# Four PSUM slots of two banks for attention, each read out for two products at once

## The chip, the cores and the metric

The kernel runs on one core of one Trainium2 chip. The metric is the device time of the program in microseconds (us). TensorE (PE) multiplies into PSUM, which has eight banks of 512 fp32 columns for each of its 128 partitions; VectorE (DVE) and ScalarE (ACT) read PSUM, GpSimd (POOL) works on the on-chip memory alone, and SyncE (SP) issues DMAs.

## The reference

Causal attention with a decay bias, for 8 batches, 8 heads, 576 positions and 64 dimensions per head; then a real part of a two-dimensional Fourier transform, a normalisation and a feed-forward layer with 2048 hidden units.

```python
scores = scale * np.matmul(q, k.transpose(0, 1, 3, 2))
cum = np.cumsum(np.maximum(s, 0.0), axis=-1)
bias = -(cum[:, :, :, None] - cum[:, :, None, :])
scores = np.where(causal, -1e9, scores + np.minimum(bias, 0.0))
scores = scores - np.max(scores, axis=-1, keepdims=True)
attn = np.exp(scores)
x = (attn / (attn.sum(-1, keepdims=True) + 1e-9)) @ v     # then heads side by side: (8, 576, 512)
u = x + np.real(np.fft.fft(np.fft.fft(x, axis=1), axis=2))
un = (u - mean(u)) / np.sqrt(var(u) + 1e-6)
out = u + np.maximum(un @ w_ch1, 0.0) @ w_ch2
```

## The kernel before

**The attention loop.** Two heads are one pair; there are 32 pairs (i), four to a batch. Iteration i of the loop does several things at once, as generators that `weave` mixes by the shares of work done: `scores(i)`, `maxes(i + 1)`, `av(i - 1)`, the preparation of the next operands (`high`, `low`), the finishing of older pairs (`recip`, `finish`), the folds and the Fourier transform (`fourier`) of an earlier batch, and a part of the conversion of the weights. TensorE's instructions keep the order in which they are written (`manual_schedule`); those of the other engines are placed by a scheduler and then run in order on each. Queue by queue, an instruction that waits holds up all behind it.

**Maxima (`maxes`).** For each head, five blocks of 128 queries (the last 64) are multiplied with all earlier keys into PSUM (tile pm, L459). The widths are 256, 256, 384 and 512 columns, and the last block takes two products of 256 and 320 columns. DVE adds the causal mask and takes the maximum of each row in one operation (L466; a second short instruction reads its accumulator); for the last block's first product it is a plain reduction (L462). The ten maxima of a pair are transposed on TensorE (pmt, L471), copied by ACT (L473) and sent by DMA into a row of the operand, so that the scores come out with the maximum taken off.

**Scores (`scores`).** Products of keys by queries, in chunks of 128 keys (table `CH`: first key, first query, number of queries, first query that counts). Each has two matmuls, one for the rounded operands and one for what the rounding left (tile ps, L491 and L492). The widths are 256 and 320 (chunk 0 in two parts), 448, 320, 256 and 256 columns; of the last two only 192 and 64 columns count. ACT takes the exponential of each into P (L495), six per head. POOL sets to zero what lies above the diagonal (L498, L501).

**Product with V (`av`).** In two column ranges, 256 (pavA) and 320 (pavB), with two and five matmuls (L523), one pass of P per chunk of keys. ACT copies each range out after its last matmul: once for the first head (L529), twice for the second (L526 for the row of sums, L527).

**PSUM.** The pool `ps` has three buffers of one bank and serves the scores, the Fourier transform, the normalisation and the hidden layer (`bank`). The pool `psm` has five and serves pm, pmt, pavA and pavB; it is closed before the feed-forward part, where four banks become the accumulators `accp`. A buffer is handed out again when its last reader is done.

**Other names.** L435 (k) subtracts the rounded keys on DVE, L438 (q) the queries on POOL; L83 to L89 convert the weights; L251 to L270 fold a batch for the transform; L284 to L336 are the transform (pzs, pzc, pyc, pys, p256) and L69 and L70 split its results; L183 is the first feed-forward product.

Of the kernel before, what the change touches and what calls it, by code (L numbers as in the profile page):

```python
# [8 lines left out]
F32 = mybir.dt.float32  # L9
# [10 lines left out]
S = 576  # L20
# [15 lines left out]
CH = [(0, 0, 576, 0), (128, 128, 448, 128), (256, 256, 320, 256), (384, 320, 256, 384), (448, 320, 256, 512)]  # L36
# [5 lines left out]
def fused_kernel(ctx, tc, qkT, vA, sP, wP, tabD, tabS, corr, out):  # L42
# [304 lines left out]
    psm = attb_ctx.enter_context(tc.tile_pool(name="psm", bufs=5, space=PSUM))  # L347
# [46 lines left out]
    trash = att.tile([128, 512], BF16, name="trash")  # L394
# [51 lines left out]
    def maxes(i):  # L446
        st = sts[i]
        qy, ky = st["qy"], st["ky"]
        M = Ms[i % 2]
        M1 = att.tile([128, 4], F32, tag="M1", name="M1", bufs=2)  # L450
        for h in range(2):
            for c in range(5):
                nq = 128 if c < 4 else 64
                nk = 128 * c + nq
                parts = [(0, max(nk, 256))] if c < 4 else [(0, 256), (256, 320)]
                col = M[:nq, 5 * h + c:5 * h + c + 1]
                for x, (k0, n) in enumerate(parts):
                    p = psm.tile([128, 512], F32, tag="m", name="pm", bufs=5)
                    nc.tensor.matmul(p[:, :n], qy[:, h, 128 * c:128 * c + 128], ky[:, h, k0:k0 + n], start=True, stop=True)  # L459
                    if len(parts) > 1 and not x:  # L460
                        first = M1[:nq, h:h + 1]
                        nc.vector.tensor_reduce(out=first, in_=p[:nq, :n], axis=AX.X, op=ALU.max)  # L462
                    else:
                        n = nk - k0
                        m0 = 512 - 128 * c + k0
                        nc.vector.tensor_tensor_reduce(out=trash[:nq, :n], in0=p[:nq, :n], in1=amask[:nq, m0:m0 + n], scale=1.0,  # L466
                                                       scalar=first if x else NEG, op0=ALU.add, op1=ALU.max, accum_out=col)
                    yield 1.0
        yield 3
        p = psm.tile([128, 512], F32, tag="m", name="pmt", bufs=5)  # L470
        nc.tensor.transpose(out=p[0:10, 0:128], in_=M, identity=ident)  # L471
        mt = att.tile([10, 128], F32R, tag="mt", name="mt", bufs=2)
        nc.scalar.copy(mt, p[0:10, 0:128])  # L473
# [3 lines left out]
    SCORES = 2 * 1600  # L477

    def scores(i):
# [3 lines left out]
        for h in range(2):  # L483
            P = attb.tile([128, PW], F32, tag="P", name="P", bufs=4)
            st["P"].append(P)
            for c, (k0, q0, nq, qk) in enumerate(CH):
                ksl = slice(k0, k0 + 128)
                parts = [(0, 256), (256, 320)] if c == 0 else [(q0, nq)]
                for a, n in parts:
                    p = bank("ps")  # L490
                    nc.tensor.matmul(p[:, :n], ky[:, h, ksl], qy[:, h, a:a + n], start=True, stop=False)  # L491
                    nc.tensor.matmul(p[:, :n], k1[:, h, ksl], q1[:, h, a:a + n], start=False, stop=True)  # L492
                    lo = max(a, qk)
                    o = POFF[c] + lo - qk
                    nc.scalar.activation(P[:, o:o + a + n - lo], p[:, lo - a:n], AF.Exp, scale=0.125)  # L495
                    if c == 3:
                        d4 = bass.AP(tensor=P.tensor, offset=P.offset, ap=[list(P.ap[0]), [576, 4], [1, 128]])
                        nc.gpsimd.affine_select(out=d4, in_=d4, pattern=[[0, 4], [1, 128]], compare_op=ALU.is_ge, fill=0.0, base=0, channel_multiplier=-1)  # L498
                    if c == 4:
# [6 lines left out]
    def av(i):  # L506
# [5 lines left out]
        for h in range(2):  # L512
            P = st["P"][h]
            vs = slice(64 * h, 64 * h + 128)
            for lo, n, tg in ((0, 256, "A"), (256, 320, "B")):
                p = psm.tile([128, 512], F32, tag="m", name="pav" + tg, bufs=5)
                cs = [c for c in range(5) if CH[c][3] < lo + n]
                for c in cs:
# [4 lines left out]
                    nc.tensor.matmul(p[:, a - lo:n], va[:, c, vs], P[:, o:o + w], start=c == 0, stop=c == cs[-1])  # L523
                    if c == cs[-1]:
                        if h:
                            nc.scalar.copy(r1[:, lo:lo + n], p[0:1, :n])  # L526
                            nc.scalar.copy(x[64:128, lo:lo + n], p[64:128, :n])  # L527
                        else:
                            nc.scalar.copy(x[:, lo:lo + n], p[:, :n])  # L529
# [107 lines left out]
    w1 = ctx.enter_context(pool("w1"))  # L637
    accp = ctx.enter_context(pool("accp", space=PSUM))
# [174 lines left out]
```

## Time and profile before

| | |
|---|---|
| median of the runs, us | 1428.55 (1426.3 to 1429.79, 3 runs) |
| the profiled execution, us | 1426.1, of which its span is 1424.4 |
| granted TensorE clock, mean | 0.97 |
| attention loop, from the start to about | 540 us |
| end of attention, first loads of weights | 540 to 720 us |
| feed-forward part | 720 us to the end |

The page gives busy time by engine, by slice and by group of instructions; the waits name the engine and line that waited, and the engine and line that ended the wait. A matmul's duration runs from its start to the end of its write, and matmuls overlap, so the distance of two starts is what one of them costs TensorE. An fp32 product (L523) shows as two matmuls.

### The profile page before, as it was taken

What the parts mean: (1) busy time and instruction counts of PE and PEld (TensorE: products, weight loads), DVE (VectorE), ACT (ScalarE), POOL (GpSimd) and SP (SyncE); (2) the same over time, 40 slices, a digit from 0 to 9 for tenths busy, and PEclk for the clock granted to TensorE, in tenths of its full rate; (3) what the DMA queues carried; (4) which work ended last, traced back from release to release, by engine and by line L of the source; (5) the groups of instructions that cost most, each with busy time, mean ns of one, the idle gap of its engine ahead of it and who ended that gap; (6) DMA issues with size and microseconds to landing.
All of it is one profiled execution on the core that took longest, in us unless ns stands there. A gap on an engine that the chain in (4) does not pass through costs nothing.

```text
span 1424.4 us, 17997 instructions
## 1 busy us (share of the span) xinstructions
PE 1305.1 (92%) x6190; PEld 1068.7 (75%) x6190; DVE 745.7 (52%) x1684; ACT 539.3 (38%) x1211; POOL 561.6 (39%) x543
## 2 busy tenths in 40 slices
PE   4887979897988887997899999999999999999998
PEld 3766868686777676775688888888888888888886
DVE  6667677877777788799833233222332223322212
ACT  4775756676665656344321121211212112121110
POOL 6445465656546566565720402204022040123300
PEclk9998999999999997999899999999999999999999
DMA  8555556565655555433200000000000000000000
GB/s 214 156 159 144 163 149 180 158 168 159 159 161 144 166 149 163 162 123 121 79 8 30 31 30 15 15 30 31 30 15 15 30 30 30 15 16 0 30 0 30
DMA packets 78230, 125.05 MB, mean 88 GB/s; under 512 B 11256, under 2 KB 36249, under 8 KB 78139
## 3 DMA queue, kind: packets, MB, share of 16 engines
q1 hardware_dynamic: 75627, 119.83, 28.4%
q0 software_dynamic: 1696, 2.50, 0.9%
q10 hardware_dynamic: 816, 1.57, 0.3%
q8 instruction: 49, 0.80, 0.2%
q14 instruction: 42, 0.34, 0.1%
HBM read 76.85 MB, written 23.07 MB: 70 GB/s over the span
## 4 chain that ended last, share of the span: by engine, by line
PE 51%; DVE 7%; POOL 2%; DMA 1%; issue 1%; ACT 1%; SPq 0%; DVEq 0%; POOLq 0%; ACTq 0%
PE h L183 25%; PE acc L198 8%; PE acc L196 8%; PE acc L197 8%; POOL we L89 1%; DVE wm L88 1%; DVE we L83 1%; DVE wm L85 1%; DVE we L87 1%; DVE wl L114 1%; ACT wh L112 1%; DMA wl<-wD 0%; POOL wl L114 0%; DVE ucl L148 0%; DVE zl L188 0%
## 5 line engine op out<-in xcount | busy, mean ns | idle before, releaser
L188 DVE SCALAR_TENSOR_TENSOR zl<-h,zh 128x512 fp32r<-128x512 f32 x144 | 98.6, 686 | 405.5 <-ACT zh L187 405.4
L187 ACT ACTIVATE zh<-h 128x512 fp32r<-128x512 f32 x144 | 85.9, 596 | 530.1 <-PE h L183 530.1
L198 PE MATMUL acc<-zl,wh 128*128 128x512 f32 x576 | 227.5, 396 | 4.9 <-DVE zl L188 4.9
L196 PE MATMUL acc<-zh,wh 128*128 128x512 f32 x576 | 227.6, 395 | 1.0 <-ACT zh L187 1.0
L197 PE MATMUL acc<-zh,wl 128*128 128x512 f32 x576 | 226.8, 394 | 0.0
L523 PE MATMUL pavB<-P,va 128*128 128x320 f32 (+2 forms) x640 | 189.1, 389 | 9.5 <-ACT stage L527 8.9
L459 PE MATMUL pm<-KQ 128*128 128x256 f32 (+3 forms) x384 | 156.5, 427 | 44.4 <-DVE Mx L466 23.1
L495 ACT ACTIVATE P<-ps 128x320 f32<-128x320 f32 (+4 forms) x384 | 145.9, 393 | 110.5 <-PE ps L492 106.8
L491 PE MATMUL ps<-KQ 128*128 128x256 f32 (+2 forms) x384 | 154.1, 404 | 24.4 <-ACT P L495 14.0
L183 PE MATMUL h<-uch,wh 128*128 128x512 f32 x576 | 159.9, 398 | 8.3 <-ACT wh L112 8.3
L183 PE MATMUL h<-uch,wl 128*128 128x512 f32 x576 | 158.1, 396 | 0.8 <-DVE wl L114 0.8
L183 PE MATMUL h<-ucl,wh 128*128 128x512 f32 x576 | 156.9, 393 | 0.0
L466 DVE CUSTOM_DVE_ANT_0 trash<-pm,amask 128x128 bf16<-128x128 f32 (+3 forms) x256 | 123.5, 482 | 34.2 <-PE pm L459 16.9
L212 POOL TENSOR_TENSOR o<-o,w 128x512 f32<-128x512 f32 x32 | 41.8, 1305 | 252.3 <-issue 218.5
L183 PEld LDWEIGHTS h<-uch,wh 128*128 128x128 f32 x576 | 108.2, 190 | 35.9 <-ACT wh L112 12.1
L198 PEld LDWEIGHTS acc<-zl,wh 128*128 128x128 f32 x576 | 108.7, 189 | 32.0 <-DVE zl L188 6.9
L183 PEld LDWEIGHTS h<-uch,wl 128*128 128x128 f32 x576 | 109.2, 190 | 26.6 <-DVE wl L114 1.2
L196 PEld LDWEIGHTS acc<-zh,wh 128*128 128x128 f32 x576 | 108.6, 188 | 26.1 <-ACT zh L187 1.8
L183 PEld LDWEIGHTS h<-ucl,wh 128*128 128x128 f32 x576 | 108.9, 189 | 24.7
L197 PEld LDWEIGHTS acc<-zh,wl 128*128 128x128 f32 x576 | 108.6, 189 | 24.7
L459 PEld LDWEIGHTS pm<-KQ 128*128 128x128 f32 x384 | 78.4, 207 | 64.7 <-DVE Mx L466 30.2
L492 PE MATMUL ps<-q,k 128*128 128x256 f32 (+2 forms) x384 | 120.5, 316 | 3.1 <-POOL q L438 3.1
(140 smaller groups left out, 2066.9 us busy)
## 6 DMA issues: line engine op xcount, KB each, us to landing
qk<-in_qkT_dram SPq DMA_DIRECT2D x32, 576.0 KB
raw<-in_wP_dram SPq DMA_DIRECT2D x64, 256.0 KB
va<-in_vA_dram SPq DMA_DIRECT2D x32, 480.0 KB
q<-KQ SPq DMA_DIRECT2D x32, 288.0 KB
k<-KQ SPq DMA_DIRECT2D x32, 288.0 KB
rb<-rd SPq DMA_DIRECT2D x64, 144.0 KB
u<-uD SPq DMA_DIRECT2D x8, 1024.0 KB
out_dram<-o SPq DMA_DIRECT2D x32, 256.0 KB
```

The lines of the kernel that those rows point to most:

```text
L183: nc.tensor.matmul(h[:, :n], a[:, j * 128:(j + 1) * 128], b[:, j, :n], start=i == 0, stop=i == 11)
L187: nc.scalar.activation(zh[:, :n], h[:, :n], AF.Relu)
L188: nc.vector.scalar_tensor_tensor(out=zl[:, :n], in0=h[:, :n], scalar=0.0, in1=zh[:, :n].bitcast(F32), op0=ALU.max, op1=ALU.subtract)
L196: nc.tensor.matmul(acc[j][:, :n], a[:, cs], y[:, :n], start=g == 0, stop=False)
L197: nc.tensor.matmul(acc[j][:, :n], b[:, cs], y[:, :n], start=False, stop=False)
L198: nc.tensor.matmul(acc[j][:, :n], a[:, cs], z[:, :n], start=False, stop=g == NF - 1)
L459: nc.tensor.matmul(p[:, :n], qy[:, h, 128 * c:128 * c + 128], ky[:, h, k0:k0 + n], start=True, stop=True)
L466: nc.vector.tensor_tensor_reduce(out=trash[:nq, :n], in0=p[:nq, :n], in1=amask[:nq, m0:m0 + n], scale=1.0, scalar=first if x else NEG, op0 ...
L491: nc.tensor.matmul(p[:, :n], ky[:, h, ksl], qy[:, h, a:a + n], start=True, stop=False)
L492: nc.tensor.matmul(p[:, :n], k1[:, h, ksl], q1[:, h, a:a + n], start=False, stop=True)
L495: nc.scalar.activation(P[:, o:o + a + n - lo], p[:, lo - a:n], AF.Exp, scale=0.125)
L523: nc.tensor.matmul(p[:, a - lo:n], va[:, c, vs], P[:, o:o + w], start=c == 0, stop=c == cs[-1])
```

## The change

PSUM becomes one pool of four slots with two banks each for everything up to the feed-forward part. There the pool is closed, and a new one of four buffers of one bank each (`ps1`) serves the hidden layer, where there were three.

- Maxima: the first three products of a head share a slot (columns 0, 256 and 512), the fourth has one, the two products of the fifth have one and are read by one operation over 576 columns on 64 partitions. The reduction L462 goes.
- Scores: chunk 0 lies in one slot across both banks and has one exponential of 576 columns; chunks 1 and 2 share a slot with an exponential each (448 and 320); chunks 3 and 4 share a bank, and one exponential of 256 columns covers both. Chunk 4's product has 64 columns in place of 256. Four exponentials per head in place of six. Both selects of POOL follow the last one.
- Product with V: one slot per head, and copies of 576 columns after the last matmul, one for the first head and two for the second.
- The share by which `scores` is woven with the rest goes from 3200 to 2880 units, as its own count falls.

```diff
-CH = [..., (384, 320, 256, 384), (448, 320, 256, 512)]
+CH = [..., (384, 320, 256, 384), (448, 512, 64, 512)]
...
-    ps = ctx.enter_context(tc.tile_pool(name="ps", bufs=3, space=PSUM))
+    ps_ctx = ExitStack()
+    ps = ps_ctx.enter_context(tc.tile_pool(name="ps", bufs=4, space=PSUM))
+    ps1 = None
+    def two(name):
+        return ps.tile([128, 1024], F32, tag="two", name=name)
     def bank(name):
-        return ps.tile([128, 512], F32, tag="bank", name=name)
+        return ps1.tile([128, 512], F32, tag="bank", name=name, bufs=4) if ps1 else two(name)
...
-    psm = attb_ctx.enter_context(tc.tile_pool(name="psm", bufs=5, space=PSUM))
...
# maxes, for block c of head h
-                for x, (k0, n) in enumerate(parts):
-                    p = psm.tile([128, 512], F32, tag="m", name="pm", bufs=5)
-                    nc.tensor.matmul(p[:, :n], ...)
-                    if len(parts) > 1 and not x:
-                        nc.vector.tensor_reduce(out=first, in_=p[:nq, :n], axis=AX.X, op=ALU.max)
-                    else:
-                        nc.vector.tensor_tensor_reduce(..., in0=p[:nq, :n], ..., accum_out=col)
+                if c in (0, 3, 4):
+                    p = two("pm")
+                at = (0, 256, 512, 0, 256)[c]
+                for k0, n in parts:
+                    nc.tensor.matmul(p[:, at + k0:at + k0 + n], ...)
                     yield 1.0
+                nc.vector.tensor_tensor_reduce(..., in0=p[:nq, at:at + nk], ..., accum_out=...)
...
# scores, for chunk c
-                    p = bank("ps")
+                if c != 2 and c != 4:
+                    p = two("ps")
+                at = (256, 64, 512, 0, 256)[c]
...
-                    nc.scalar.activation(P[:, o:o + a + n - lo], p[:, lo - a:n], AF.Exp, scale=0.125)
+                    if c == 3 or c == 0 and not a:
+                        yield 2 * n / 2.4
+                        continue
+                    if c == 4:
+                        nc.scalar.activation(P[:, POFF[3]:POFF[3] + 256], p[:, 64:320], AF.Exp, scale=0.125)
+                    else:
+                        nc.scalar.activation(P[:, POFF[c]:POFF[c] + nq], p[:, at:at + nq], AF.Exp, scale=0.125)
...
# av
-            for lo, n, tg in ((0, 256, "A"), (256, 320, "B")):
-                p = psm.tile([128, 512], F32, tag="m", name="pav" + tg, bufs=5)
+            p = two("pav")
+            for lo, n in ((0, 256), (256, 320)):
...
-                            nc.scalar.copy(x[:, lo:lo + n], p[:, :n])
+                            nc.scalar.copy(x, p[:, 256:832])
...
+    ps_ctx.close()
+    ps1 = ctx.enter_context(pool("ps1", space=PSUM))
```

What this makes of the order, at three places. The number behind a name is the buffer that was asked for, so two products with one number lie in one slot; what a row waits for stands in brackets.

TensorE at the start of a pair's maxima, before: every pm is a buffer of its own.

```order
L459 MATMUL pm_5099<-KQ0_119 128x256 [waits DMAHW5_49]
L315 MATMUL pys_5071<-ssin0_85,zs0_4699 128x290
L315 MATMUL pys_5071<-ssin1_86,zs0_4699 128x290
L315 MATMUL pys_5071<-ssin0_85,zs1_4700 128x290
L491 MATMUL ps_5115<-KQ2_121 128x256 [waits DMAHW2_49,Activation_49]
L492 MATMUL ps_5115<-q1_4900,k1_4901 128x256 [waits DMAHW4_49,DMAHW3_49,Pool_49]
L459 MATMUL pm_5119<-KQ0_119 128x256
L491 MATMUL ps_5122<-KQ2_121 128x320 [waits Activation_49]
L492 MATMUL ps_5122<-q1_4900,k1_4901 128x320
L523 MATMUL pavA_5096<-P_4916,va_4888 128x128
L459 MATMUL pm_5128<-KQ0_119 128x384 [waits DVE_49]
```

The same place after:

```order
L464 MATMUL pm_4467<-KQ0_116 128x256 [waits DMAHW5_49,Activation_49]
L320 MATMUL pys_4442<-ssin0_85,zs0_4114 128x290
L320 MATMUL pys_4442<-ssin1_86,zs0_4114 128x290
L320 MATMUL pys_4442<-ssin0_85,zs1_4115 128x290
L493 MATMUL ps_4482<-KQ2_118 128x256 [waits DMAHW2_49,PE_49,Activation_49]
L494 MATMUL ps_4482<-q1_4291,k1_4292 128x256 [waits DMAHW4_49,DMAHW3_49,Pool_49]
L464 MATMUL pm_4467<-KQ0_116 128x256 [waits DVE_49]
L493 MATMUL ps_4482<-KQ2_118 128x320
L494 MATMUL ps_4482<-q1_4291,k1_4292 128x320
L528 MATMUL pav_4465<-P_4307,va_4281 128x128
L464 MATMUL pm_4467<-KQ0_116 128x384 [waits DVE_49]
```

The rows stand as before, but the second and third product of the head now wait for DVE's maximum of the one ahead of them in the same slot (4467).

TensorE at the third to fifth product of the second head, before:

```order
L459 MATMUL pm_5191<-KQ0_119 128x384 [waits DVE_49]
L491 MATMUL ps_5194<-KQ2_121 128x256 [waits Activation_49]
L492 MATMUL ps_5194<-q1_4900,k1_4901 128x256
L459 MATMUL pm_5199<-KQ0_119 128x512 [waits DVE_49]
L523 MATMUL pavB_5134<-P_4916,va_4888 128x192
L491 MATMUL ps_5207<-KQ2_121 128x256 [waits Activation_49]
L492 MATMUL ps_5207<-q1_4900,k1_4901 128x256
L459 MATMUL pm_5212<-KQ0_119 128x256 [waits DVE_49]
```

and after:

```order
L464 MATMUL pm_4532<-KQ0_116 128x384 [waits DVE_49]
L493 MATMUL ps_4550<-KQ2_118 128x256 [waits Activation_49]
L494 MATMUL ps_4550<-q1_4291,k1_4292 128x256
L464 MATMUL pm_4554<-KQ0_116 128x512 [waits DVE_49]
L528 MATMUL pav_4465<-P_4307,va_4281 128x192
L464 MATMUL pm_4562<-KQ0_116 128x256 [waits DVE_49]
```

The last score product has moved behind the fifth maximum's. With the product with V, the scores and a transform product in three slots, pm_4554 gets the slot of pm_4532 and pm_4562 that of pm_4554: their waits are for the maximum of the product three and two rows ahead. Before, the waits of these rows were for maxima five buffers back.

DVE at the start of a pair's maxima, after (before, the same rows stand in the same order):

```order
L439 TENSOR_TENSOR k1_4470<-qk_4102,KQ0_116 64x576 [waits DMAHW7_49,DMAHW3_49,PE_49]
L439 TENSOR_TENSOR k1_4470<-qk_4102,KQ0_116 64x576
L466 ISA trash_134,Mx1_126<-pm_4467,amask_129 128x128 [waits DVE_49,PE_49]
L466 ISA Mx1_126 128x1
L88 TENSOR_SCALAR we_4357<-raw_4355 128x256 [waits DMAHW7_49,DMAHW6_49,Pool_49]
L90 TENSOR_SCALAR wm_4354<-raw_4355 128x256
L93 SCALAR_TENSOR_TENSOR wm_4354<-raw_4355,wm_4354 128x256 [waits DVE_49]
L92 SCALAR_TENSOR_TENSOR we_4357<-raw_4355,we_4357 128x256 [waits Activation_49]
L466 ISA trash_134,Mx1_126<-pm_4467,amask_129 128x256 [waits PE_49]
```

Nothing moved here; what is new is that the products of the fence above wait for these maxima, behind the subtraction of keys and the conversion of a piece of weights.

More of the change, by code (lines that the diff above doesn't have):

```diff
@@ L455, in maxes @@
                 parts = [(0, max(nk, 256))] if c < 4 else [(0, 256), (256, 320)]
[L456 to L467 removed]
+                if c in (0, 3, 4):
+                    p = two("pm")
+                at = (0, 256, 512, 0, 256)[c]
+                for k0, n in parts:
+                    nc.tensor.matmul(p[:, at + k0:at + k0 + n], qy[:, h, 128 * c:128 * c + 128], ky[:, h, k0:k0 + n], start=True, stop=True)
                     yield 1.0
+                nc.vector.tensor_tensor_reduce(out=trash[:nq, :nk], in0=p[:nq, at:at + nk], in1=amask[:nq, 640 - nk - 128 + nq:640 - 128 + nq], scale=1.0,
+                                               scalar=NEG, op0=ALU.add, op1=ALU.max, accum_out=M[:nq, 5 * h + c:5 * h + c + 1])
         yield 3
[L470 removed]
+        p = two("pmt")
         nc.tensor.transpose(out=p[0:10, 0:128], in_=M, identity=ident)
```

25 lines of the change are left out of this document (11 added, 14 removed).

## The prediction

> **What bounds the kernel now.** First the busy shares, then two stretches: most of the attention loop (100 to 540 us) and the feed-forward part (720 us to the end). Columns: stretch and length, then busy us and count for TensorE (PE), its weight loads, DVE, ACT and POOL, granted clock, DMA share, GB/s.
>
> ```profile
> PE 1305.1 (92%) x6190; PEld 1068.7 (75%) x6190; DVE 745.7 (52%) x1684; ACT 539.3 (38%) x1211; POOL 561.6 (39%) x543
> ...
> 100.00:540.00 440.00, 379.82 (x2153) 321.38 (x2151) 327.02 (x921) 277.93 (x695) 257.50 (x264) 0.95 0.57 159
> ...
> 720.00:1424.00 704.00, 698.77 (x3029) 568.30 (x3027) 197.90 (x263) 122.62 (x208) 138.83 (x103) 1.00 0.06 21
> ```
>
> In the feed-forward part TensorE has no gaps to speak of (698.77 of 704). In attention it is busy for 379.82 of 440 us, DVE for 327 (74%), ACT for 278 (63%): no engine is full. TensorE runs its instructions in a written order, so the loop loses or wins through what TensorE waits for. The waits from 60 to 540 us (who waits, for whom, us, times, longest):
>
> ```profile
> PE pm L459 <- DVE Mx L466: 22.4, 11, 5.5
> PE ps L491 <- ACT P L495: 14.0, 17, 2.2
> PE pavB L523 <- ACT stage L527: 8.5, 12, 1.6
> ...
> PE pm L459 <- ACT stage L527: 2.4, 4, 0.7
> ```
>
> All four are waits for a PSUM buffer to be read out. Each pair of heads has one transpose of its maxima, copied by ACT; count, first and last start give the length of an iteration:
>
> ```profile
> L473 ACT CAST mt<-pmt x30: 237/239/257, 47.5 to 524.0; 10x128 fp32r<-10x128 f32 x30
> ```
>
> (524.0 - 47.5)/29 = 16.4 us per pair. The sum below is per pair, times 29, against the profiled execution of 1426.1 us, which is 2.4 below the median of the runs shown.
>
> **The change part by part: the readers.** The forms that are merged (count, then busy us, mean ns):
>
> ```profile
> L495 ACT ACTIVATE P<-ps 128x320 f32<-128x320 f32 x116 | 50.5, 435 | 32.8 <-PE ps L492 32.1
> ...
> L466 DVE CUSTOM_DVE_ANT_0 trash<-pm,amask 128x512 bf16<-128x512 f32 x56 | 38.0, 679 | 7.4 <-PE pm L459 3.1
> ...
> L495 ACT ACTIVATE P<-ps 128x448 f32<-128x448 f32 x58 | 31.6, 545 | 22.0 <-PE ps L492 21.6
> ...
> L466 DVE CUSTOM_DVE_ANT_0 trash<-pm,amask,M 64x320 bf16<-64x320 f32 x56 | 30.0, 535 | 8.8 <-PE pm L459 3.2 <-PE ps L492 0.5
> ...
> L466 DVE CUSTOM_DVE_ANT_0 trash<-pm,amask 128x256 bf16<-128x256 f32 x56 | 23.2, 415 | 5.2 <-PE pm L459 1.8
> L462 DVE TENSOR_REDUCE M<-pm 64x1 f32<-64x256 f32 x56 | 23.0, 411 | 0.9 <-PE pm L459 0.8
> L495 ACT ACTIVATE P<-ps 128x256 f32<-128x256 f32 x59 | 22.9, 389 | 5.7 <-PE ps L492 4.9
> L495 ACT ACTIVATE P<-ps 128x192 f32<-128x192 f32 x58 | 19.0, 328 | 27.5 <-PE ps L492 27.0
> ...
> L495 ACT ACTIVATE P<-ps 128x64 f32<-128x64 f32 x58 | 13.0, 224 | 7.8 <-PE ps L492 6.9
> L529 ACT COPY stage<-pavB 128x320 f32<-128x320 f32 x30 | 12.8, 426 | 0.4
> ...
> L529 ACT COPY stage<-pavA 128x256 f32<-128x256 f32 x29 | 10.9, 376 | 0.0
> ```
>
> Exponentials: (545-389)/192 = 0.81 ns a column, so 576 columns take 545+128x0.81 = 649 ns in place of 389+435, and 256 take 389 in place of 328+224: 338 ns less per head. Copies of the product with V: (426-376)/64 = 0.78, so 576 take 626 in place of 802, once for the first head and twice for the second: 528 ns less per pair. ACT sheds 2x338+528 = 1.2 us per pair, 35 us in the loop. At 63% busy this is not on the path by itself; it can shorten only the waits for ACT, 14.0+8.5+2.4 = 24.9 us. Against it, a buffer with two products comes free later. I take 10 us of gain; the ends are 0 and 25.
>
> The Trainium skill ("Perfetto Trace Analysis", Optimizing Scalar/DVE Operations) says that grouping pays if the engine is saturated, and that where Scalar or Vector is not, but causes bubbles elsewhere, breaking instructions up may let work complete sooner. By that rule the 10 us would not come, and the sum would be 10 higher.
>
> The last maximum: a reduction (411) and one over 320 columns (535) become one over 576: (679-415)/256 = 1.03 ns a column, so 535+264 = 799 ns, which can begin only after the second product. DVE sheds 0.15 us per head, off the path.
>
> **The narrower product.** The last score product shrinks from 256 to 64 columns, four matmuls per pair. How far apart 256-column ones start:
>
> ```profile
> 313.75 0.28 PE L491 MATMUL ps<-KQ 128*128 128x256 f32 x1
> 313.87 0.28 PE L492 MATMUL ps<-q,k 128*128 128x256 f32 x1
> ```
>
> 0.12 us. No row has an fp32r product below 256 columns: in proportion it saves 0.09, at worst nothing. 128 of them make 0 to 11.5 us, on TensorE's own path. I take 6, the middle.
>
> **The shared buffers.** Before, the maxima and the product with V have five buffers and scores and transform three; each product has its own. Now all share four slots, and a product that goes into a slot in use waits for the reader of the one before it. I lay the new order of the section on the change over one pair of the trace. First TensorE (start, duration), then DVE:
>
> ```profile
> 308.51 0.28 PE L459 MATMUL pm<-KQ 128*128 128x256 f32 x1
> ...
> 309.06 0.42 PE L459 MATMUL pm<-KQ 128*128 128x384 f32 x1
> ...
> 312.10 0.28 PE L459 MATMUL pm<-KQ 128*128 128x256 f32 x1
> ...
> 312.52 0.28 PE L459 MATMUL pm<-KQ 128*128 128x256 f32 x1
> ...
> 313.57 0.34 PE L459 MATMUL pm<-KQ 128*128 128x384 f32 x1
> ...
> 313.99 0.39 PE L459 MATMUL pm<-KQ 128*128 128x512 f32 x1
> 314.22 0.49 PE L523 MATMUL pavB<-P,va 128*128 128x192 f32 x2
> 314.41 0.41 PE L491 MATMUL ps<-KQ 128*128 128x256 f32 x1
> ```
>
> ```profile
> 308.31 0.29 DVE L466 CUSTOM_DVE_ANT_0 trash<-pm,amask 128x128 bf16<-128x128 f32 x1
> 308.53 0.08 DVE L466 DVE_READ_ACCUMULATOR2_ANT Mx<- 128x1 f32 x1
> 308.82 0.42 DVE L466 CUSTOM_DVE_ANT_0 trash<-pm,amask 128x256 bf16<-128x256 f32 x1 [0.21 <-PE pm L459]
> ...
> 313.54 0.27 DVE L466 CUSTOM_DVE_ANT_0 trash<-pm,amask 128x128 bf16<-128x128 f32 x1
> 313.75 0.07 DVE L466 DVE_READ_ACCUMULATOR2_ANT Mx<- 128x1 f32 x1
> ...
> 314.04 0.35 DVE L466 CUSTOM_DVE_ANT_0 trash<-pm,amask 128x256 bf16<-128x256 f32 x1
> ...
> 314.54 0.56 DVE L466 CUSTOM_DVE_ANT_0 trash<-pm,amask 128x384 bf16<-128x384 f32 x1
> ```
>
> DVE starts 0.03 us after a product's end when it is free (308.51+0.28 to 308.82). First head: the second product, at 308.51, would wait for the first one's maximum, read out at 308.53+0.08: 0.10. Its own maximum then ends at 308.61+0.28+0.03+0.42+0.08 = 309.42; the third, at 309.06+0.10, waits 0.26. Together 0.36.
>
> Second head: its second product, due at 312.52+0.36, shares the slot of the first, whose maximum ends at 313.75+0.07 = 313.82, since DVE is behind: 0.94 lost, 1.30 so far. The third, at 313.57+1.30 = 314.87, finds its forerunner read out (313.82+0.28+0.03+0.42+0.08 = 314.63). The fourth takes the third's slot: due at 313.99+1.30 = 315.29, free at 314.87+0.34+0.03+0.56+0.08 = 315.88: 0.59, 1.89 so far. The fifth takes the fourth's and now stands right behind the product with V: due at 314.41+1.89 = 316.30, free at 315.88+0.39+0.03+0.68+0.08 = 317.06: 0.76. So 2.65 us in this pair, some 2.7 with the longer last maximum. The five old buffers covered this: these three maxima end 1.6 to 2.0 us after their products start, and TensorE goes on.
>
> Times 29: +78 us. Were both heads like the first, 0.72 per pair, +21; both like the second, 4.6, +133. I take the pair as it is.
>
> Behind a waiting product stand scores and products with V in TensorE's order, so ACT and POOL wait with it. The second pair of score products in a slot waits likewise for the first's exponential: at 318.00 the 448-column product ends and 319.02 is when the next comes.
>
> ```profile
> 318.00 0.36 PE L492 MATMUL ps<-q,k 128*128 128x448 f32 x1
> 319.02 0.55 PE L491 MATMUL ps<-KQ 128*128 128x320 f32 x1
> ```
>
> 0.36+0.03+0.545 is 0.94 of the 1.02 us: it just fits if ACT is free, and a 649 ns exponential stands in front. I take 0.2 us per pair, +6; ends 0 and 15.
>
> The same skill page (Matmuls) says that independent groups should rotate through different banks, so that the reading of one overlaps the next one's matmuls. The trace before agrees: the second product starts at 308.51, 0.10 before the first is read out. The page gives no price.
>
> Costed at nothing: both selects on POOL now follow the joint exponential, but their reader, the product with V, comes an iteration later. The feed-forward products get four buffers for three, and TensorE waits there for weights, not for a buffer:
>
> ```profile
> L183 PE MATMUL h<-uch,wh 128*128 128x512 f32 x576 | 159.9, 398 | 8.3 <-ACT wh L112 8.3
> ```
>
> The sum: +78 +6 -6 -10 = +68; 1426.1+68 = 1494 us.
>
> **The rivals.** (a) The waits fall largely into time that TensorE loses anyway, 60 of 440 us, because DVE is in front of its queue: the low end, +21+6-6-10, some +5 to +30, so 1431 to 1456. For it: DVE is idle for a quarter of the loop. Against it: it is behind by that much just where the maxima come in a row.
>
> (b) Worse: both heads like the second (+133), so 1549, and TensorE's clock falls below the 0.95 of the loop as it idles; at 0.90 its 380 us cost 20 more, 1569. For it: the feed-forward part, which never idles, has 1.00.
>
> The skill's "TensorE: Matmul & The Clock Gate" (Part 1: The HAM clock gate) has the clock halved after an idle window of about 3.4 us; stalls of under 1 us, as worked out here, would not reach that.
>
> (c) Faster: merged readers end the 24.9 us of waits for ACT and the narrow products save 6, while the maxima, in one slot after another, add little. It decides at (24.9+6)/29 = 1.07 us of new waits per pair; at 0.5, 14.5 in all, the time is 1426-31+15 = 1410. Against it: the first head's 0.36 needs no queue at all on DVE, and the second's is 2.3.
>
> (d) The gains and the waits cancel, around 1 us per pair: 1426. That the change would not do what it says is excluded by the order: the merged readers are there.
>
> **How the numbers follow.** Likeliest, 60%: 1494, with a range of its own from 1456 to 1549. (a) 13%, (b) 12%, (c) 9%, (d) 6%. Runs of this kernel spread over 0.25%, so a change within 0.3% can't be told from none. Slower 85%, same 6%, faster 9%. The range of 1434 to 1568 leaves out (c), (d) and the edges of (a) and (b), some 2 in 10.
>
> **What would show it.** Iterations of about 18.8 us in place of 16.4; the wait of the maxima's products for DVE grown from 22 to some 100 us in many short pieces, now also ended by the maximum just before; ACT's exponentials 8 per pair of 649, 545, 435 and 389 ns; starts of the 64-column products nearer than 0.12 us. The prediction is wrong if the maxima's products wait less than 1 us per pair, if DVE reads the slots out as fast as they fill, or if the clock moves more than the waits. The feed-forward part should last as long as before.

## The result, and the profile after

The changed kernel takes 1524.61 us (median of 4 runs, 1523.02 to 1526.11) against 1427.47 for the kernel before on the same chip (4 runs, 1426.3 to 1429.79): ratio 1.0678, 95% interval 1.0658 to 1.0698. It is slower by 97 us; forecast were 68 us more, 1494. The profiled execution took 1523.63 us, its span 1521.8, at a mean granted clock of 0.965.

The busy shares, and the stretches of the attention loop and of the feed-forward part (columns as in the prediction):

```profile
PE 1354.1 (89%) x6190; PEld 1076.3 (71%) x6190; DVE 727.3 (48%) x1620; ACT 517.2 (34%) x987; POOL 542.9 (36%) x543
...
100.00:600.00 500.00, 410.04 (x2103) 319.92 (x2102) 302.30 (x853) 255.31 (x500) 230.53 (x252) 0.94 0.48 135
820.00:1521.00 701.00, 696.18 (x3018) 566.15 (x3016) 197.35 (x262) 122.01 (x207) 138.41 (x103) 1.00 0.06 22
```

The last row is the later feed-forward part, and TensorE works there as before: 696 of 701 us busy. In the loop DVE is now busy for 60% instead of 74%, ACT for 51% instead of 63%: both are less busy, and TensorE gets less done per us all the same. The copies of the transposed maxima give the iteration (count, durations in ns, first and last start in us):

```profile
L472 ACT CAST mt<-pmt x30: 238/238/256, 54.1 to 609.6; 10x128 fp32r<-10x128 f32 x30
```

(609.6-54.1)/29 = 19.16 us per pair; before it was 16.43. The 97.4 us between the two spans lie in three places: 6.6 before the first of these copies (54.1 against 47.5), 79.0 in the 29 pairs, and 11.8 from the last copy to the end (912.2 against 900.4).

The longest waits of TensorE in the loop, 60 to 640 us (the one of `mu`, at 629 us, lies behind it):

```profile
PE pm L464 <- DVE Mx L466: 48.0, 59, 5.1
PE ps L493 <- ACT stage L532: 8.7, 8, 1.8
PE mu L128 <- ACT th L74: 8.5, 1, 8.5
PE pzc L297 <- DVE Mx L466: 6.0, 12, 0.7
PE ps L493 <- ACT P L501: 4.5, 7, 1.0
PE pzs L289 <- ACT stage L532: 4.2, 6, 0.7
```

The maxima's products wait for DVE 59 times in place of 11. Two rows of the same view with all engines in it show both halves of it, first before (60 to 540 us), then after:

```profile
PEld pm L459 <- DVE Mx L466: 26.5, 15, 5.6
DVE trash L466 <- PE pm L459: 14.0, 27, 2.1
...
DVE trash L466 <- PE pm L464: 84.3, 154, 1.6
PEld pm L464 <- DVE Mx L466: 82.4, 115, 5.3
```

TensorE's weight loads for these products wait 82 us for DVE, and DVE waits 84 us for the products: with few slots left for the maxima the two engines work more in turn. DVE's work is nearly what it was (335 us in the 29 pairs, 350 before); its share falls because the loop is longer, though TensorE waits for it more. New in kind are `pzs` and `pzc`: the transform's products, which take a whole two-bank slot for one bank of columns, wait for readers of the attention.

One pair, at the place in the program of the prediction's walk, TensorE's rows of the second head; in brackets the idle time ahead of a row and what ended it:

```profile
362.01 0.39 PE L464 MATMUL pm<-KQ 128*128 128x256 f32 x1 [0.45 <-DVE Mx L466]
...
364.95 0.50 PE L464 MATMUL pm<-KQ 128*128 128x512 f32 x1 [0.42 <-DVE Mx L466]
...
366.24 0.39 PE L464 MATMUL pm<-KQ 128*128 128x256 f32 x1 [0.47 <-DVE Mx L466]
...
366.87 0.19 PE L493 MATMUL ps<-KQ 128*128 128x64 f32 x1
366.91 0.27 PE L494 MATMUL ps<-q,k 128*128 128x64 f32 x1
367.01 0.41 PE L528 MATMUL pav<-P,va 128*128 128x64 f32 x2
```

The walk had 0.94 at the second product, 0.59 at the fourth and 0.76 at the fifth. Here it is 0.45 at the first, 0.42 and 0.47. DVE's rows of the same time show why they are shorter:

```profile
363.21 0.42 DVE L466 CUSTOM_DVE_ANT_0 trash<-pm,amask 128x256 bf16<-128x256 f32 x1 [0.48 <-PE pm L464]
...
364.33 0.56 DVE L466 CUSTOM_DVE_ANT_0 trash<-pm,amask 128x384 bf16<-128x384 f32 x1 [0.69 <-PE pm L464]
```

DVE stands ready when the second and the third product come. I read this as TensorE's earlier waits having let it catch up; it is one pair. The merged readers, by form (count, busy us, mean ns):

```profile
L501 ACT ACTIVATE P<-ps 128x576 f32<-128x576 f32 x64 | 41.7, 652 | 25.6 <-PE ps L494 23.4 <-POOL P L506 1.4 <-issue 0.2
L501 ACT ACTIVATE P<-ps 128x448 f32<-128x448 f32 x64 | 34.8, 544 | 58.5 <-PE ps L494 58.0
L501 ACT ACTIVATE P<-ps 128x320 f32<-128x320 f32 x64 | 27.9, 436 | 38.0 <-PE ps L494 37.6
L499 ACT ACTIVATE P<-ps 128x256 f32<-128x256 f32 x64 | 24.6, 385 | 22.2 <-PE ps L494 21.1
...
L534 ACT COPY stage<-pav 128x576 f32<-128x576 f32 x32 | 20.4, 637 | 2.7 <-PE pav L528 1.6 <-POOL P L506 0.8
```

652, 544, 436 and 385 ns were forecast as 649, 545, 435 and 389, and the copy of 637 as 626. The largest maximum, over 576 columns, takes 748 ns, forecast as 799.

A second reading sums, over TensorE's rows, the time from one matmul's start to the next less its columns at 2.4 per ns (the rate that the kernel's own `yield 2 * n / 2.4` counts with; the two matmuls of an fp32 product with twice their columns each), and puts what is left to the product that starts late. What is left holds more than waits: at a clock of 1.00, in the feed-forward part, 512 columns start 0.231 us apart and not 0.213, and time at a lower clock counts in it too. In the 29 pairs:

| us | before | after | |
|---|---|---|---|
| columns | 345.5 | 336.5 | -9 |
| lost at pm | 22.1 | 65.3 | +43 |
| lost at ps | 61.7 | 71.6 | +10 |
| lost at the product with V | 32.3 | 42.6 | +10 |
| lost at the transform | 13.4 | 39.0 | +26 |

(Lost in all, small entries with it: 130.9 and 219.1.)

The clock is a part of this. In the trace's rows it is either 1.00 or 0.50, in stretches of 3.4 us and multiples of it; in the 29 pairs it stands at 0.50 for 61 us in all, and for 41 before. Twenty us more at half the clock cost at most some 10 of the 79, an estimate that takes TensorE as the limit throughout.

### The profile page after: what moved, and what is told of

Same layout as the page of the kernel before. It is cut to its first block, busy times and chain, and to the rows that moved or that the text cites. A ratio compares the mean times of both kernels' runs of the same rounds, so it can differ in the third digit from the quotient of the medians.

```text
span 1521.8 us, 17622 instructions
## 1 busy us (share of the span) xinstructions
PE 1354.1 (89%) x6190; PEld 1076.3 (71%) x6190; DVE 727.3 (48%) x1620; ACT 517.2 (34%) x987; POOL 542.9 (36%) x543
## 4 chain that ended last, share of the span: by engine, by line
PE 48%; DVE 6%; POOL 2%; issue 1%; ACT 1%; DMA 1%; SPq 0%; DVEq 0%; POOLq 0%; ACTq 0%
PE h L188 23%; PE acc L203 8%; PE acc L201 8%; PE acc L202 8%; POOL we L94 1%; DVE wm L93 1%; DVE wm L90 1%; DVE we L92 1%; DVE we L88 1%; DVE wl L119 1%; POOL wl L119 1%; ACT wh L117 1%; PE pys L320 0%; DMA wl<-wD 0%; PE pyc L311 0%
## 5 line engine op out<-in xcount | busy, mean ns | idle before, releaser
L528 PE MATMUL pav<-P,va 128*128 128x320 f32 (+4 forms) x896 | 259.2, 385 | 6.9 <-ACT P L499 3.6
L464 PE MATMUL pm<-KQ 128*128 128x256 f32 (+3 forms) x384 | 164.8, 443 | 70.3 <-DVE Mx L466 55.0
L466 DVE CUSTOM_DVE_ANT_0 trash<-pm,amask 128x128 bf16<-128x128 f32 (+4 forms) x320 | 173.0, 540 | 103.3 <-PE pm L464 94.4
L493 PE MATMUL ps<-KQ 128*128 128x256 f32 (+3 forms) x384 | 152.7, 398 | 27.5 <-ACT stage L532 8.7
L528 PEld LDWEIGHTS pav<-P,va 128*128 128x128 f32 x896 | 148.8, 200 | 14.2 <-issue 7.9
L501 ACT ACTIVATE P<-ps 128x576 f32<-128x576 f32 (+2 forms) x192 | 104.3, 544 | 122.1 <-PE ps L494 119.0
```

Source lines behind the costliest of these rows:

```text
L464: nc.tensor.matmul(p[:, at + k0:at + k0 + n], qy[:, h, 128 * c:128 * c + 128], ky[:, h, k0:k0 + n], start=True, stop=True)
L466: nc.vector.tensor_tensor_reduce(out=trash[:nq, :nk], in0=p[:nq, at:at + nk], in1=amask[:nq, 640 - nk - 128 + nq:640 - 128 + nq], scale=1. ...
L493: nc.tensor.matmul(p[:, o:o + n], ky[:, h, ksl], qy[:, h, a:a + n], start=True, stop=False)
L501: nc.scalar.activation(P[:, POFF[c]:POFF[c] + nq], p[:, at:at + nq], AF.Exp, scale=0.125)
L528: nc.tensor.matmul(p[:, 256 + a:256 + lo + n], va[:, c, vs], P[:, o:o + w], start=c == 0, stop=c == cs[-1])
```

## The experiments

Theory: the loss is the number of slots. Four in place of eight leave one or two for the maxima, and what DVE and ACT take to read a slot out passes on to TensorE. Rivals: that two products stand in one slot, one behind the other's reader, whatever the number; that single-bank work (the transform) loses by taking double slots; that the merged readers cost by themselves; and, after the first four runs, that the new order of the rows does. Differences below are ratio minus one, times 1428.5 us, since the kernel before came out a little differently beside each set of runs (1427 to 1431 us).

| kernel | buffers | order | ratio, 95% interval | difference, us |
|---|---|---|---|---|
| changed kernel | 4 double | new | 1.0678 (1.0658 to 1.0698) | +97 |
| e1_narrow | 3 + 5 | new | 1.0061 (1.0042 to 1.0080) | +9 |
| e2_own_slot | 4 double | new | 1.0503 (1.0473 to 1.0533) | +72 |
| e3_transform_banks | 3 double, 2 single | new | 1.1063 (1.1037 to 1.1089) | +152 |
| e4_scores_two | 2 double, 4 single | new | 1.0209 (1.0182 to 1.0237) | +30 |
| e5_before_short | 3 + 5 | old | 1.0002 (0.9979 to 1.0025) | 0 |
| e6_after_short | 4 double | new | 1.0436 (1.0409 to 1.0463) | +62 |
| e7_narrow_old_order | 3 + 5 | old | 1.0038 (1.0022 to 1.0053) | +5 |
| e8_before_new_order | 3 + 5 | new | 1.0051 (1.0033 to 1.0069) | +7 |
| e9_after_old_order | 4 double | old | 1.0571 (1.0547 to 1.0595) | +82 |
| e10_four_single | 4 single | old | 1.0730 (1.0708 to 1.0752) | +104 |
| e11_six_buffers | 3 + 3 | old | 1.0335 (1.0310 to 1.0360) | +48 |
| e12_narrow_only | 3 + 5 | old | 1.0003 (0.9985 to 1.0020) | 0 |

**The number of buffers, with nothing merged.** e10 and e11 change the kernel before only in its pools.

```diff
# e11
-    psm = ... tile_pool(name="psm", bufs=5, space=PSUM)
+    psm = ... tile_pool(name="psm", bufs=3, space=PSUM)
# e10: no psm; pm, pmt, pavA and pavB come from bank() too
-    ps = ... tile_pool(name="ps", bufs=3, space=PSUM)
+    ps = ... tile_pool(name="ps", bufs=4, space=PSUM)
```

> The kernel before with one pool of four single banks for everything, in place of three and five; products, readers and order as before. The number of buffers is that of the changed kernel, but each product has its own reader and none stands with another in a slot. If the number of buffers alone made the loss: at or above the changed kernel, since each product now takes a buffer where two or three shared one: 1525 to 1620. If it was the sharing (a product waits for the reader of its partner, a reader for both products): 1440 to 1490. I expect the first.

> The kernel before with three buffers in place of five for the maxima and the product with V; the other three, all products, readers and the order stay. With eight buffers the time is 1428, with four single ones for everything 1533. If each buffer taken away costs alike, 1480; if the fifth and fourth were mostly idle and only the last ones bite, 1435 to 1460. I expect the second, near the 1461 of the kernel with the scores in two double slots, which has six buffers too.

Four: 1532.9 us, +104. Six: 1479.08 us, +48, in the first case of its expectation, not in the one I held. e10 came as expected. So each buffer taken away costs 24 us on the way from eight to six, and 28 from six to four, a nearly straight line where I had looked for a bend. It rests on three points, and the step to four also joins the two pools; seven and five buffers were not run. Where the loss shows depends on who shares with whom. e11's waits, 60 to 570 us:

```profile
PE pm L459 <- ACT stage L527: 67.8, 27, 9.0
PE ps L491 <- ACT P L495: 10.8, 5, 2.6
PE pm L459 <- DVE Mx L466: 5.0, 23, 0.4
```

and e10's, 60 to 650 us:

```profile
PE pmt L470 <- ACT P L494: 15.7, 6, 3.8
PE pm L458 <- ACT stage L526: 15.5, 15, 1.6
PE ps L490 <- DVE Mx L465: 12.1, 8, 6.1
PE ps L490 <- ACT P L494: 8.3, 22, 1.1
```

With three buffers next to the product with V, the maxima wait about once per pair for a copy of that product (L527), and hardly for DVE. With four for all, the waits spread over every user. The engine that is named changes with the pools.

**Scores in double slots, the rest single.** e4 takes the changed kernel's `scores` with two slots of two banks, and gives the maxima, the product with V and the transform of the kernel before four single banks.

```diff
# against the kernel before; scores() and CH as in the changed kernel, pm, pmt, pavA and pavB from bank()
-    ps = ... tile_pool(name="ps", bufs=3, space=PSUM)
+    ps = ... tile_pool(name="ps", bufs=4, space=PSUM)
-    psm = ... tile_pool(name="psm", bufs=5, space=PSUM)
+    psc = ... tile_pool(name="psc", bufs=2, space=PSUM)      # [128, 1024], for scores() alone
```

> Half of the change: the scores use two slots of two banks with one exponential for each block, and the last product of 64 columns, as in the changed kernel; the maxima, the product with V and the transform have single banks and readers of their own as before, four banks in all. So there are six buffers where the kernel before had eight and the changed one has four. If the shortage of buffers for the maxima makes the loss, half of the buffers that were lost are back, and the maxima's products no longer stand in one slot with their forerunner: 1440 to 1475. If the merged exponentials and their slots make the loss (second product in a slot behind the first one's exponential), the time stays above 1495.

1460.73 us, as the theory had it: +30 with six buffers. That is 18 us less than e11 with six buffers, in which nothing is merged (e4 stands in the new order, has the narrow product and shares out its pools differently, so the 18 us are not those of the merging alone).

**A slot for each maximum's product.**

```diff
-                if c in (0, 3, 4):
-                    p = two("pm")
+                p = two("pm")
```

> The changed kernel, but each of the first three blocks' maxima products takes a slot of its own, as the product's own buffer was before; only the last two blocks still share one. Two theories. Same slot one after another (a product waits because its forerunner in the same slot must be read out first): most of what the maxima's products lost more than before goes, some 43 us by the trace, of which I expect 30 to 45 to show, so 1480 to 1495. Too few slots (there are four for everything, and whoever takes one more takes it from another): the waits move from the maxima to the scores and the product with V, and the time stays within 10 us of the changed kernel, 1515 to 1535. I hold the second for somewhat likelier, since DVE still has to read each slot before it returns.

1504.85 us, between the two: 25 us of the 97 come back. The waits, 60 to 620 us:

```profile
PE pm L463 <- DVE Mx L465: 35.6, 42, 5.1
PE pm L463 <- ACT stage L531: 9.6, 10, 1.5
```

The wait for DVE falls from 48.0 to 35.6, and 9.6 of waits for ACT's copies take part of its place. By the second reading the maxima's products lose 60.0 us, against 65.3 in the changed kernel, and the scores 60.3 against 71.6. So both theories hold in part: fewer products stand behind a partner, and a slot more for the maxima is a slot less for others, though it costs less than I thought. Most of the gain does not show at the maxima's own products.

**Single banks for the transform.**

```diff
-    ps = ps_ctx.enter_context(tc.tile_pool(name="ps", bufs=4, space=PSUM))
+    ps = ps_ctx.enter_context(tc.tile_pool(name="ps", bufs=3, space=PSUM))
+    pf = ps_ctx.enter_context(tc.tile_pool(name="pf", bufs=2, space=PSUM))   # bank() takes these
```

> The changed kernel with three two-bank slots in place of four, and two single banks for the products of the transform and the normalisation, which use one bank each. The transform's products lost 25.6 us more in the loop of the changed kernel than before, which my forecast had not in its sum. If this is a cost of their own (single-bank work that stands in line for two-bank slots), it goes: -15 to -25 us, 1500 to 1510. If the number of slots is what counts, the attention products lose with three slots more than the transform wins: 1530 to 1580. I take the second: the transform's waits are then a symptom of the same shortage.

1583.16 us, +152, a little beyond the second case. Its waits, 60 to 700 us:

```profile
PE pm L465 <- DVE Mx L467: 74.5, 120, 2.4
PE ps L494 <- ACT stage L533: 19.6, 20, 2.1
PE ps L494 <- ACT P L500: 9.1, 16, 0.9
```

The transform's own loss (39 us, by the second reading) falls to about 17, and the three slots left make the maxima wait 120 times. I take its waits in the changed kernel for a share of the same shortage; e3 takes a slot away as well, so it does not show this apart.

**DVE's reading time.** The maxima read the last 128 columns of each block only, in both kernels.

```diff
# e6; e5 does the same at L462 and L466 of the kernel before
+                e = nk - 128
-                nc.vector.tensor_tensor_reduce(out=trash[:nq, :nk], in0=p[:nq, at:at + nk], ...
+                nc.vector.tensor_tensor_reduce(out=trash[:nq, e:nk], in0=p[:nq, at + e:at + nk], ...
```

> The kernel before, with DVE reading only the last 128 columns of each block for the maximum, and the last 128 of the last block's first product, in place of up to 512 (so the maxima are over a part of the keys). TensorE's products, the slots and the order stay. It is the yardstick for the same edit in the changed kernel. DVE's reading falls by some 2.4 us per pair, but TensorE waits for the maxima 22 us in the loop: a gain of 5 to 20, 1408 to 1423.

> The changed kernel with the same short reading of the maxima (the last 128 columns of each block, so over a part of the keys). If the time that DVE takes to read a product out is what the shared slots pass on to TensorE, as my hand walk had it, most of the 65 us that the maxima's products lose goes, far more than in the kernel before: a gain of 35 to 60, 1465 to 1490. If the slots are simply too few for all users (scores, product with V and transform as well), the gain is like that of the kernel before plus a little, 10 to 25: 1500 to 1515.

In the kernel before: nothing (1430.95 against 1431.34 us), though I expected 5 to 20. In the changed one: 1493.7 us, 35 us less by the ratios, the low end of the gain of the first case, and a little above its 1490. The loss of the maxima's products falls from 65.3 to 44.5 us by the second reading, not most of it. The loop of before and of e5, then of the changed kernel and of e6:

```profile
47.50:524.04 476.54, 412.87 (x2341) 349.05 (x2341) 349.88 (x1007) 304.96 (x760) 268.34 (x278) 0.96 0.57 157
```

```profile
49.00:529.00 480.00, 417.09 (x2351) 356.40 (x2350) 295.41 (x1012) 304.74 (x762) 271.81 (x278) 0.94 0.57 156
```

```profile
54.10:609.64 555.54, 457.07 (x2342) 355.30 (x2341) 335.14 (x955) 285.43 (x558) 256.30 (x278) 0.94 0.48 135
...
45.74:579.57 533.83, 448.40 (x2342) 354.30 (x2343) 270.52 (x954) 285.51 (x559) 261.21 (x278) 0.94 0.51 140
```

DVE sheds 54 us in e5 (349.88 to 295.41), and the loop is no shorter. In e6 it sheds 65 (335.14 to 270.52), and the loop is 22 us shorter. There the weight loads of the maxima's products wait 54.9 us in place of 80.0 (60 to 600 us in both), while DVE waits more for TensorE, 122.1 us in place of 82.6:

```profile
DVE trash L467 <- PE pm L464: 122.1, 175, 2.0
PEld pm L464 <- DVE Mx L467: 54.9, 83, 5.3
```

About 1 us per head of DVE's reading is covered with eight buffers; with four, a little more than half of what is shed comes off the time. This is the shortage at the place that the prediction walked.

**The narrow product and its joint exponential.** e1 takes chunks 3 and 4 of the changed kernel alone; e7 is e1 with the share and the last chunk's count of the kernel before; e12 keeps even the own buffer and the own exponential.

```diff
# e1, e7, e12
-CH = [..., (448, 320, 256, 512)]
+CH = [..., (448, 512, 64, 512)]
# e1, e7: chunk 4 goes into chunk 3's bank, one exponential for both, POOL's selects after it
+    nc.scalar.activation(P[:, POFF[3]:POFF[3] + 256], p[:, 64:320], AF.Exp, scale=0.125)
# e1
-    SCORES = 2 * 1600
+    SCORES = 2 * 1440
# e7, e12
-                    yield 2 * n / 2.4
+                    yield 2 * max(n, 256) / 2.4
```

> The kernel before with one piece of the change: the last score product has 64 columns in place of 256 and stands in the same bank as the fourth one, and one exponential of 256 columns reads both. All buffers stay as before (five for the maxima and the product with V, three for scores and transform). If the change's loss is in the sharing of the four slots, this piece alone keeps its gain: 128 narrower matmuls and one ACT instruction less per head, -5 to -12 us against before, so 1415 to 1422. If a reader that covers two products already costs by itself (the buffer is released later, and the first of two products waits for its partner), the time is that of before or above it, 1427 to 1440.

> The narrow product with its joint exponential alone cost 7.6 us where I expected a gain of 5 to 12, though TensorE streamed 9.8 us less in the loop. With it went the share by which the scores are woven with the rest (2880 for 3200), which sets TensorE's written order. Here the narrow product stays and the share goes back to 3200 (and to 256 columns for the last chunk), so the rows stand in the order of the kernel before. If the new order made the loss: faster than before, 1415 to 1422. If the joint exponential made it (the product with V of the next iteration finds P later, since both selects of POOL now follow the last exponential): 1432 to 1440 as without this edit.

> The kernel before, in its own order, with the last score product of 64 columns in place of 256; its own buffer, exponential and select stay, so nothing is joined. TensorE streams some 9 us less. If the joint exponential took that gain in the earlier runs: 1416 to 1424. If TensorE's clock takes it (the granted clock of the loop fell from 0.96 to 0.92 in the profile of the narrow product in the old order): 1425 to 1436.

None gains: 1438.52, 1434.5 and 1432.1 us; all three came out in their second ranges, so the gain of 5 to 12 us did not come. By the second reading e12 streams 8 us of columns less than before, and loses 15 us more, spread over scores and product with V; e7 loses 8 more in the loop and 8 more behind it. A part of this is no wait for a buffer. From the start of the narrow matmuls to that of the row behind them, the trace has 12.5 us in the 29 pairs of e12 and 18.1 before: 5.6 less, not 8. The second of two narrow matmuls starts as little as 0.03 us after the first, but the row behind the second one, of another product, never less than 0.108 us later (0.113 before, behind 256 columns). What holds that row is open. Which waits take the rest isn't settled, since runs of the kernel before go from 1424 to 1436 us; nor is the clock's share: the mean was 0.96 in the loop of before, 0.95 in that of e12 and 0.92 in that of e7, where it stood at one half for 72 us in place of 41, and over the runs of before a lower clock goes only loosely with a longer time (correlations of -0.57, -0.37 and -0.44 in three sets of runs). That 128 narrower products gain nothing is measured. The joint exponential, with the bank that it reads and the selects behind it, costs some 5 us (e7 against e12; their intervals just part, and the lower clock of e7 may have a part in it).

**The order.** e8 is the kernel before, e9 the changed kernel, each with the other's share for `scores` and count of the last chunk.

```diff
# e8
-    SCORES = 2 * 1600
+    SCORES = 2 * 1440
-                    yield 2 * n / 2.4
+                    yield 2 * (n if c < 4 else 64) / 2.4
# e9
-    SCORES = 2 * 1440
+    SCORES = 2 * 1600
-                    yield 2 * n / 2.4
+                    yield 2 * max(n, 256) / 2.4
```

> The kernel before with nothing but the changed kernel's weave: 2880 units for the scores, the last chunk counted as 64 columns. All products, buffers and readers as before. If the order makes the loss of the narrow product: slower than before, by 10 to 17 us, 1438 to 1445. If the joint exponential makes it: as before, within 4 us, 1424 to 1433.

> The changed kernel with the weave of the kernel before (3200 units, the last chunk counted as 256 columns). If the order costs the same in the changed kernel as in the one before: 1505 to 1515. If four slots make waits of their own wherever the rows stand: within 8 us of the changed kernel, 1516 to 1533.

The new order costs 7 us in the kernel before (1435.42, between the two cases of e8) and 15 in the changed one (1509.41 against 1524.61, the first case of e9). e9's loop runs from 52.5 to 604.5 us by the copies of its maxima:

```profile
L472 ACT CAST mt<-pmt x30: 237/238/255, 52.5 to 604.5; 10x128 fp32r<-10x128 f32 x30
```

That is 19.03 us per pair, near the 19.16 of the changed kernel (4 us in 29 pairs); from there to the end it takes 902.4 us in place of 912.2. In these profiles most of the order's price lies behind the loop, in the kernel before too: there the pairs take 2 us more (478.5 against 476.5) and the part behind them 7 (907.4 against 900.4). Over all these kernels that part takes 904 to 914 us in the new order and 899 to 909 in the old. The two ranges overlap, so where the price lies is not shown.

In one order, four double slots (e9, +82) beat four single ones (e10, +104) by 23 us: sharing slots and readers, with the narrow product, is worth something when there are only four. It is far from the price of the four that are gone. No kernel here beats the one before. The Trainium skill ("Perfetto Trace Analysis", Matmul Optimizations) asks that all eight PSUM banks be leveraged. e11, with two of them idle, agrees (+48); e9 uses all eight, in four slots, and loses 82: what counts in these runs is how many parts can be handed out and come free on their own.

## Why the prediction was right, and where its sum was not

The direction, the place of the loss and the range held; 1494 was 31 us short, and it came as near as it did by luck: terms that were too large and too small offset each other. Step by step:

- **Slots for the maxima, +78.** The place is right: waits for DVE grown from 22.4 us in 11 pieces to 48.0 in 59, ended by the maximum just before, and e6 and e2 show that DVE's reading (35 us) and the sharing of one slot by three products (25 us) bear on the loss, not to be added. The size is not: some 100 us of this wait were forecast, and by the second reading pm lost 43 us more, against 78. The walk took DVE's lateness from the trace of before (0.94 at the second head's second product), but in the pair shown after the change each wait is 0.4 to 0.5 us, and DVE is ready for two of the products. The walk moved only TensorE, and here it overstated. (The maxima that it has ending 1.6 to 2.0 us after their products start do so after 1.5 to 2.0 by its rows; its sum does not use that.)
- **The transform, 0 in the sum.** This is the step that was missing: +26 us in the loop. The prediction dealt the four slots to maxima, scores and product with V, and named the transform only as a holder of one.
- **Scores +6 and merged ACT readers -10.** Together they should have given 4; scores and product with V lost 20 us more. The forms of ACT took the time forecast for each, but its busy time in the loop fell by 19.5 us (304.96 to 285.43) and not by 35: the working summed durations, and neighbouring ones overlap (before, those of the loop sum to 327 us). And with every slot in use a copy or an exponential releases it for whoever is next (`ps` behind L532, 8.7 us). The joint exponential, with its bank, costs some 5. The rule of the Trainium skill ("Perfetto Trace Analysis", Optimizing Scalar/DVE Operations) that the prediction weighed, that grouping pays on a saturated engine, fits this one: ACT is at 64% in the loop of before (304.96 of 476.54), and the joint one does not pay. It does not cover the 23 us by which shared slots and readers beat single ones at four.
- **The narrower product, -6.** In the rows above the second starts 0.04 us after the first and the next product 0.10 after the second; over the 29 pairs the columns fell by 9 us, the distances of starts by 4 in the changed kernel and 5.6 in e12, near the 6 taken (for 128 matmuls, of which the 29 pairs hold 116). The kernel's time did not fall: e12.
- **Outside the 29 pairs, 0 in the sum.** +6.6 before and +11.8 behind. For the pairs alone the forecast was +68 and 18.8 us per pair, the trace +79 and 19.16: the terms above cancel, and 18 of the 31 us lie outside the pairs. e9, in the old order, takes 10 of these 11.8 less; the prediction read the order and did not cost it.
- **Nothing on POOL, feed-forward as before.** Held for POOL: ACT's exponentials wait 1.4 us for its selects. The feed-forward part runs as before once it is under way, 696 of 701 us busy, but from its first product to the end it takes 859.8 us in place of 852.0, 7.8 of the 11.8 above. The other kernels lie between 849.2 and 864.4, so the buffers need not be the reason.
- **The rivals.** The cover of (a) and the gain of (c) did not come; (c) decided at 1.07 us of new waits per pair, and what is newly lost is 88/29 = 3.0. Of (b) the clock went from 0.96 to 0.94 in the loop, not to 0.90. But the argument against (b), that only a whole window of some 3.4 us idle would halve the clock, does not fit this trace: from 276.10 to 279.52 us TensorE is busy for 1.66 of 3.42 us, with no idle time above 1.8 us, and the next 3.41 us are at 0.50. The same follows 2.17 busy of 3.40 us up to 293.2, where no idle time is above 1.5. What sets the clock was not tested.

## What to carry over

Before PSUM buffers are traded for larger ones, count all users of the pool, and price a slot by taking some away in the kernel as it is: here two buffers cost 48 us and four 104, and the waits then named different engines. An engine that looks idle for a quarter of the loop can still set the time once its reading is no longer covered by spare buffers: 54 us less of DVE's work were worth nothing with eight, and 65 us less were worth 35 with four. And when a change shortens one stream of a woven order, move the order alone as well: it cost 7 and 15 us here.

## What the runs showed beyond that

Of two fp32r matmuls of 64 columns in a row the second started as little as 0.03 us after the first, but the next product never less than 0.107 us after the second, where it is 0.113 behind 256 columns. So three quarters fewer columns saved less than a third of the time between starts, and 128 of them made no difference that could be measured (ratio 1.0003), in a loop where TensorE is busy for 87% of the time by the profile.

The mean granted clock in the loop lay between 0.91 (e3) and 0.96 (before) over these kernels. It is a mix of 1.00 and 0.50 in stretches of 3.4 us and multiples, and did not follow how busy TensorE was: e7 was at 0.92 with TensorE busy for 88% of its loop, the changed kernel at 0.94 with 82%.
